# A linear-attention and softplus-MLP kernel: x^T's factor made by Pool, the softplus table loaded first, and a hand-set plan with new positions

## Chip, cores and metric

One core of one Trainium2 chip. The metric is the device time of one execution in microseconds (us). Engines: PE (TensorE, matmuls; PEld are its weight loads), DVE (VectorE), ACT (ScalarE), POOL (GpSimd), SP (SyncE, which here only issues DMA transfers).

## The reference

```python
q, k, v: (8, 8, 576, 64)    g_norm: (64,)    w_in: (512, 2048)    w_out: (2048, 512)
kv  = einsum('bhsd,bhse->bhde', k, v)
out = einsum('bhsd,bhde->bhse', q, kv)
rms = sqrt(mean(out * out, axis=-1, keepdims=True) + 1e-06)
y   = (out / rms * g_norm).astype(float32)
x   = y.transpose(0, 2, 1, 3).reshape(4608, 512)
h   = x @ w_in
g   = maximum(h, 0) + log1p(exp(-abs(h)))          # softplus
return (g @ w_out).astype(float32)
```

The inputs w_in and w_out arrive with twice the width of float32 (64 bits each); the kernel makes float32 of them itself.

## The kernel before

**The two halves.** The attention half works by batch (8) and by tile of 128 tokens (36 tiles). For a batch, `kv_of` loads k and v in four pairs of 256 KB and two tails (L483, L481), multiplies them into one bank of PSUM (L494, "kv group") and copies the result into a block-diagonal tile, kv_diag (L498). For a tile of tokens, `rows` brings q with its rows turned (by PE and an ACT copy for the first two batches, L563 and L570; by DVE from the third on, L538), multiplies with kv_diag (L508, "out_rows"), squares on ACT (L576), sums on DVE (L513), takes the root on POOL (L516, L517) and scales on DVE (L520). The result is turned (L525 on PE for the first 12 tiles) to x^T.

**Three-part numbers.** Every operand of the MLP half is split into three float32r parts, so that three fast matmuls give nearly the exact product. For x^T this is `split`: a high part on ACT (L437, scaled by the column g_down), a low part on DVE (L440, which reads g_col) and a third on DVE (L444). g_col holds g_norm twice, 128 rows; g_down is g_col times a constant near 1.

**Weights.** `weight` loads a chunk of 128 rows or columns of w_in or w_out as raw 64-bit words (512 KB, L275), in one of two raw buffers. ACT squares the high words (L286) to find which are zero, DVE makes float32 of the words in six steps (L290, L294, L299, L307, L312, L316; L299 reads ACT's square, and L312 is the last that reads raw), ACT collects a check sum (L303). `divide` then makes the three parts: high on ACT (L348), low on DVE (L351), low scaled up on ACT (L355), and the third part: for the first four chunks through PE (L366 with ident_r, L367 with minus_r, which is minus the identity, and L370 on ACT), later on DVE and ACT (L358, L362).

**The MLP half** runs over 12 blocks of 384 tokens and 16 chunks of d_ff, in three phases that share the chunks out; 192 steps in all. A step is one h (12 matmuls, L646), softplus and high part on ACT (L666, L668), low and third part on DVE (L657, L661), and three sums of 128 tokens (9 matmuls, L653). At the end of a phase a block's sums go to DRAM or to the output (`leave`).

**What sets the order.** Nothing is ordered by the program's text except the set-up at L725 to L736. All the rest are tasks with an engine, an estimated duration, the tasks they follow, the buffers they take and give, and a position. `Plan.order` plays the program through once on the host with these estimates: at each step it takes, among the tasks that could begin within SOON (150 ns) of the earliest, the one with the lowest position. It starts with all engines free at 0 (`engine_free`) and the transfers free at 0 (`dma_free`). The positions of the early weights, loads and tiles come from the list P0 (its first 8 entries for the conversion of the first chunks, the next 8 for their loads, 11 for the attention half, 13 for later chunks). Every engine then runs its own list strictly in the planned order, and an instruction that waits holds up all that stand behind it on its engine; SP's list of transfers too. Where the plan has PE idle ahead of the first h, it puts in a filler matmul (`warm`, L762), not before BEGIN (4000 ns) of the plan's clock.

**The set-up** before: ACT issues two small loads of g_norm (L726), makes g_down (L727), loads softplus's table (L728) and later makes minus_r (L732). POOL makes an identity, DVE copies it to ident_r (L731) and sets constants (L733 to L736).

Of the kernel before, what the change touches and what calls it, by code (L numbers as in the profile page):

```python
# [13 lines left out]
ALU = mybir.AluOpType  # L14
# [8 lines left out]
DOWN_G = 1.0 - 0.99 * 2.0 ** -13  # L23
# [17 lines left out]
class Plan:  # L41
# [2 lines left out]


    HANDOVER = {"PE": 250, "ACT": 120, "DVE": 120, "POOL": 150, "SP": 0}
    BEGIN = 4000
    SOON = 150

# [17 lines left out]
    def order(self):  # L67
        waiting = {id(t): len(t.after) + (t.follows is not None) for t in self.tasks}
        users = {}
        for t in self.tasks:  # L70
            for a in t.after + ([t.follows] if t.follows else []):
                users.setdefault(id(a), []).append(t)
        ready = {}
        for t in self.tasks:
            if not waiting[id(t)]:
                t.ready = 0
                ready.setdefault(t.engine, []).append(t)
        free = {r: [(0, i) for i in range(n)] for r, n in self.rings.items()}
        engine_free = {"PE": 0, "ACT": 0, "DVE": 0, "POOL": 0, "SP": 0}
        dma_free = 0  # L80
        last_read = {}
        done, left = [], len(self.tasks)
        while left:
            best = None
            for engine, tasks in ready.items():
                options = []
                for t in tasks:
                    at = max(engine_free[engine], t.ready)
                    if t.size:
                        at = max(at, dma_free - 2500)  # L90
                    for i, s in enumerate(t.take):
                        others = sum(u.ring == s.ring for u in t.take[:i])
                        if len(free[s.ring]) <= others:
                            break
                        at = max(at, sorted(free[s.ring])[others][0])
                    else:
                        options.append((at, t))
                if not options:
                    continue
                first = min(at for at, _ in options)  # L100
                at, t = min(((at, t) for at, t in options if at <= first + self.SOON),
                            key=lambda o: (o[1].pos, o[0]))
                if engine == "PE" and self.spare and self.spare[-1].start is None:
                    ring, run, ns, _ = self.spare
                    begin = max(engine_free["PE"], self.BEGIN, min(free[ring])[0] if free[ring] else at)
                    if begin + ns <= at:
                        s = Slot(ring)
                        at, t = begin, Task("PE", ns, lambda s=s: run(s), [], 0.0, [s], [s], 0)
                        s.readers = 1
                if best is None or at < best[0]:  # L110
                    best = (at, t)
            if best is None:
                raise RuntimeError("the plan is stuck at " + str([(e, t.pos, [s.ring for s in t.take if not free[s.ring]]) for e, ts in ready.items() for t in ts][:20]))
            at, t = best
            if t in ready[t.engine]:
                ready[t.engine].remove(t)
                left -= 1
            for s in t.take:
                place = min(free[s.ring])
                free[s.ring].remove(place)  # L120
                s.place = place[1]
            t.start = at
            engine_free[t.engine] = at + t.ns
            t.end = at + t.ns + self.HANDOVER[t.engine]
            if t.size:
                dma_free = max(dma_free, at + t.ns) + t.size
                t.end = dma_free + 2000
            for s in t.give:
                s.readers -= 1
                last_read[id(s)] = max(last_read.get(id(s), 0), t.end)  # L130
                if not s.readers:
                    free[s.ring].append((last_read[id(s)], s.place))
            for u in users.get(id(t), ()):
                waiting[id(u)] -= 1
                if not waiting[id(u)]:
                    u.ready = max([a.end for a in u.after] + ([u.follows.start] if u.follows else []), default=0)
                    ready.setdefault(u.engine, []).append(u)
            done.append(t)
        return sorted(done, key=lambda t: t.start)
# [3 lines left out]
def kernel(  # L143
# [24 lines left out]
    nc = tc.nc  # L168
# [14 lines left out]
    PLACES = 8  # L183
    LAST = PHASES[-1]

    P0 = [-72.5, -0.2, -57.8, -8.7, -11.6, -12.0, -21.4, 2.2, -57.5, -32.8, -36.2, -10.7, -28.2, 0.3,
          -3.2, -2.2, 0.5, -17.5, 12.5, 9.5, 5.5, 6.5, -2.0, 2.5, 2.5, 33.5, 12.5, 14.5, 8.5, 44.5,
          49.5, 68.5, 52.5, 73.0, 96.5, 99.5, 115.5, 110.5, 114.5, 8.5]
    CONVERT, FETCH, EARLY, LATER = P0[:8], P0[8:16], P0[16:27], P0[27:]
    BY_PE = 12  # L190
    AT_ONCE = 2 * TB
# [8 lines left out]
    ident = ident_r.bitcast(F32)  # L200
    minus_r = const.tile([P, P], F32R, name="minus_r")
    g_col = const.tile([P, 1], F32, name="g_col")
    g_down = const.tile([P, 1], F32, name="g_down")
# [520 lines left out]

    for e in range(2):  # L725
        nc.scalar.dma_start(out=g_col[e * D:(e + 1) * D], in_=g_norm.rearrange("(d one) -> d one", one=1))  # L726
    nc.scalar.mul(g_down, g_col, DOWN_G)  # L727
    nc.scalar.preload_act_table_set("softplus")  # L728
    scratch = kv_diag[0][:, 0]
    make_identity(nc, scratch)  # L730
    nc.vector.tensor_copy(ident_r, scratch)  # L731
    nc.scalar.mul(minus_r, ident, -1.0)  # L732
    nc.vector.memset(half, -0.5)  # L733
    nc.vector.memset(big, 2.0 ** 30)
    for x in kv_diag + tails:
# [62 lines left out]
```

## Time and profile before

| | us |
|---|---|
| median of 9 runs (lowest, highest) | 913.12 (912.41, 913.68) |
| the profiled execution's own time | 913.05 |
| its span in the trace | 911.3 |
| PE busy | 898.6 (99%) |
| of it h matmuls (L646, 2304) | 434.3 |
| of it sums (L653, 1728) | 434.1 |
| of it filler (L762, 36) | 15.6 |
| DVE busy | 625.5 (69%) |
| ACT busy | 415.4 (46%) |
| POOL busy | 80.6 (9%) |
| HBM traffic | 143 GB/s over the span |

A line of the timeline has the start, the duration (both in us), the engine, the line of the kernel, the operation, what it writes and reads, the shapes and the count; in brackets how long the engine stood idle before it and what ended that. The windows give, for a stretch, each engine's busy time and count, the granted TensorE clock (1.00 is full), the busy share of the DMA engines (a little over 1 is possible) and GB/s. A line of the waits says who waited for whom, how long in total, how often, and the longest.

### The profile page before, as it was taken

The numbers are of one execution on the slowest core, as the hardware profiler recorded it, in microseconds if no ns is written. First come the engines' busy times: TensorE is split into PE (matmuls) and PEld (weight loads), VectorE is DVE, ScalarE is ACT, GpSimd is POOL, SyncE is SP. The second block draws the span as 40 slices with busy tenths as digits, with TensorE's granted clock in tenths as the row PEclk, the third lists the DMA queues.
The fourth block names the chain that finished last, engine by engine and source line by source line (L and its number), as shares of the span: only waits on it lengthen the run. The fifth ranks groups of instructions, "written<-read, shape, count | busy, mean of one in ns | idle before, by whom it ended". The sixth has DMA issues, their size and how long they took to land.

```text
span 911.3 us, 13889 instructions
## 1 busy us (share of the span) xinstructions
PE 898.6 (99%) x5134; PEld 802.5 (88%) x5134; DVE 625.5 (69%) x1055; ACT 415.4 (46%) x799; POOL 80.6 (9%) x78
## 2 busy tenths in 40 slices
PE   6999999999999999999999999999999999999998
PEld 4788989988889999999999899989999899999997
DVE  5887888775658887688756878888434555555553
ACT  4876556443435557454433545546323333333331
POOL 0333312212123200000000000000000000000000
PEclk7999999999999999999999999999999999999999
DMA  8999999579692644356333454642330433333323
GB/s 229 250 247 255 241 192 223 91 194 169 182 148 64 167 128 139 116 160 200 104 104 127 127 175 139 218 140 94 104 101 4 138 105 105 105 104 105 104 71 103
DMA packets 211444, 131.47 MB, mean 144 GB/s; under 512 B 102320, under 2 KB 185264, under 8 KB 211376
## 3 DMA queue, kind: packets, MB, share of 16 engines
q1 hardware_dynamic: 211216, 130.58, 53.2%
q8 instruction: 40, 0.66, 0.3%
q14 instruction: 28, 0.23, 0.1%
q10 hardware_dynamic: 160, 0.00, 0.0%
HBM read 91.75 MB, written 38.80 MB: 143 GB/s over the span
## 4 chain that ended last, share of the span: by engine, by line
PE 97%; ACT 1%; DVE 1%; DMA 1%; issue 0%; ACTq 0%; DVEq 0%
PE h L646 44%; PE s L653 44%; PE o L508 3%; PE o L494 2%; DMA g_col<-in_g_norm_dram 1%; PE tp L563 1%; PE h L762 0%; PE tp L525 0%; PE h L367 0%; PE s L508 0%; PE h L366 0%; DVE xv L440 0%; DVE m L351 0%; ACT L728 0%; ACT L727 0%
## 5 line engine op out<-in xcount | busy, mean ns | idle before, releaser
L646 PE MATMUL h<-xv,w 128*128 128x384 f32 x2304 | 434.3, 337 | 0.0
L653 PE MATMUL s<-w,gv 128*128 128x512 f32 x1728 | 434.1, 395 | 0.0
L646 PEld LDWEIGHTS h<-xv,w 128*128 128x128 f32 x2304 | 406.6, 188 | 15.1
L653 PEld LDWEIGHTS s<-w,gv 128*128 128x128 f32 x1728 | 319.6, 188 | 59.9 <-issue 0.5
L666 ACT ACTIVATE g<-h 128x384 f32<-128x384 f32 x192 | 94.3, 491 | 396.5 <-PE h L646 388.6
L657 DVE TENSOR_TENSOR gv<-g,gv 128x384 fp32r<-128x384 f32 x192 | 106.7, 556 | 187.2 <-ACT gv L668 186.3
L661 DVE SCALAR_TENSOR_TENSOR gv<-gv 128x384 fp32r<-128x384 f32 x192 | 106.9, 557 | 5.9
L668 ACT ACTIVATE gv<-g 128x384 fp32r<-128x384 f32 x192 | 100.8, 525 | 20.4 <-PE s L653 12.4
L440 DVE SCALAR_TENSOR_TENSOR xv<-m,g_col,xv 128x512 fp32r<-128x512 f32 x102 | 75.8, 743 | 1.3 <-ACT xv L437 1.1
L444 DVE SCALAR_TENSOR_TENSOR xv<-xv 128x512 fp32r<-128x512 f32 x108 | 74.5, 690 | 2.7
L437 ACT ACTIVATE xv<-m,g_down 128x512 fp32r<-128x512 f32 x102 | 70.0, 711 | 3.2 <-DMA m<-x 2.8
L517 POOL TENSOR_TENSOR r<-r,half 128x8 f32<-128x8 f32 x36 | 65.7, 1824 | 3.0
L693 DVE SCALAR_TENSOR_TENSOR m<-s,scale,m 128x512 f32<-128x512 f32 x24 | 17.9, 746 | 30.1 <-PE s L653 30.1
L508 PE MATMUL o<-kv_diag,m 128*128 128x128 f32 (+1 forms) x296 | 37.1, 276 | 0.3 <-ACT kv_diag L498 0.3
L508 PEld LDWEIGHTS o<-kv_diag,m 128*128 128x128 f32 (+1 forms) x296 | 35.0, 179 | 2.4 <-issue 0.9
L516 POOL TENSOR_SCALAR r<-r 128x8 f32<-128x8 f32 x36 | 14.3, 396 | 235.2 <-DVE r L513 235.0
L513 DVE TENSOR_REDUCE r<-x 128x8 f32<-128x512 f32 x36 | 24.4, 679 | 11.3 <-ACT x L576 11.3
L693 DVE SCALAR_TENSOR_TENSOR m<-s,m 128x512 f32<-128x512 f32 x36 | 23.6, 684 | 9.5 <-PE s L653 9.4
L494 PEld LDWEIGHTS o<-m,m 128*64 128x64 f32 x512 | 18.7, 148 | 11.7 <-issue 6.0
L520 DVE TENSOR_TENSOR x<-o,r 128x512 f32<-128x512 f32 x33 | 22.6, 686 | 7.8 <-POOL r L517 7.5
L299 DVE SCALAR_TENSOR_TENSOR m<-sq,m 128x512 f32<-128x512 bf16 x32 | 22.0, 687 | 8.7 <-ACT sq L286 7.4
L303 ACT ACTIVATE sq<-sq,big 128x512 bf16<-128x512 bf16 x32 | 22.9, 716 | 10.0 <-DVE m L299 9.9
(66 smaller groups left out, 436.8 us busy)
## 6 DMA issues: line engine op xcount, KB each, us to landing
m<-x SPq DMA_DIRECT2D x102, 256.0 KB, 4.6
part<-m SPq DMA_DIRECT2D x72, 256.0 KB, 2.7
m<-part SPq DMA_DIRECT2D x72, 256.0 KB, 3.8
raw<-in_moe_w_in_dram SPq DMA_DIRECT2D x16, 512.0 KB, 5.4
m<-in_k_dram SPq DMA_DIRECT2D x32, 256.0 KB, 4.6
m<-in_v_dram SPq DMA_DIRECT2D x32, 256.0 KB, 4.8
raw<-in_moe_w_out_dram SPq DMA_DIRECT2D x16, 512.0 KB, 4.9
qa<-in_q_dram SPq DMA_DIRECT2D x24, 288.0 KB, 6.5
```

The costliest lines, as they stand in the source:

```text
L437: nc.scalar.activation(cols(0, F32R), x.tile, func=AF.Identity, scale=g_down)
L440: nc.vector.scalar_tensor_tensor(out=cols(1, F32R), in0=x.tile, scalar=g_col, in1=cols(0), op0=ALU.mult, op1=ALU.subtract)
L444: nc.vector.scalar_tensor_tensor(out=cols(2, F32R), in0=cols(1), scalar=-RADIX, in1=cols(0), op0=ALU.mult, op1=ALU.add)
L508: nc.tensor.matmul(y[r0:r0 + n, p::NP], lhsT=qT.tile[:, p, r0:r0 + n], rhs=kv_diag[b % 2][:, p].rearrange("r (h d) -> r h d", d=D), start= ...
L517: nc.gpsimd.tensor_tensor(out=r.tile, in0=r.tile, in1=half, op=ALU.pow)
L646: nc.tensor.matmul(hp, lhsT=w_in.tile[:, i, kd * P:(kd + 1) * P], rhs=xv.tile[:, i, kd], start=(m == 0), stop=(m == 3 * KD - 1))
L653: nc.tensor.matmul(mine[i].tile, lhsT=gv.tile[:, m, i * P:(i + 1) * P], rhs=w_out.tile[:, m], start=(c == cs[0] and m == 0), stop=(c == cs ...
L657: nc.vector.tensor_tensor(out=gv.tile[:, 1], in0=g.tile, in1=gv.tile.bitcast(F32)[:, 0], op=ALU.subtract)
L661: nc.vector.scalar_tensor_tensor(out=gv.tile[:, 2], in0=f32[:, 1], scalar=-RADIX, in1=f32[:, 0], op0=ALU.mult, op1=ALU.add)
L666: a = add("ACT", 490, lambda: nc.scalar.activation(new(g, [P, NT]), h.tile, func=AF.Softplus, scale=1.0 + E), [a], s, [g], [h])
L668: a = add("ACT", 530, lambda: nc.scalar.activation(new(gv, [P, 3, NT], F32R)[:, 0], g.tile, func=AF.Copy, scale=DOWN), [a], s, [gv])
L693: a = add("DVE", 700, lambda: nc.vector.scalar_tensor_tensor(out=new(ot, [P, d_model]), in0=bank.tile, scalar=(scale if ph == LAST else 1. ...
```

## The change

Three things: g_down is made by POOL and minus_r by DVE, both of which ACT made before, so that ACT's first instruction behind the two loads is softplus's table; the plan starts with the engines free at the times of READY and the transfers free at 1500 ns, in place of 0; and the list of positions P0 has new numbers.

```diff
+    READY = {"PE": 2500, "ACT": 2500, "DVE": 4000, "POOL": 2500, "SP": 700}
...
-        engine_free = {"PE": 0, "ACT": 0, "DVE": 0, "POOL": 0, "SP": 0}
-        dma_free = 0
+        engine_free = dict(self.READY)
+        dma_free = 1500
...
-    P0 = [-72.5, -0.2, -57.8, -8.7, -11.6, -12.0, -21.4, 2.2, -57.5, -32.8, -36.2, -10.7, -28.2, 0.3,
-          -3.2, -2.2, 0.5, -17.5, 12.5, 9.5, 5.5, 6.5, -2.0, 2.5, 2.5, 33.5, 12.5, 14.5, 8.5, 44.5,
-          49.5, 68.5, 52.5, 73.0, 96.5, 99.5, 115.5, 110.5, 114.5, 8.5]
+    P0 = [-83.5, -6.7, -71.3, -7.7, -12.6, -28.5, -9.9, 1.7, -54.5, -35.3, -53.7, -10.7, -25.7, -1.2,
+          -3.7, -2.2, 0.5, -14.0, 12.5, 9.5, 5.5, 6.0, -2.0, 2.5, 2.5, 19.0, 0.5, 14.5, 8.5, 44.5, 49.5,
+          68.0, 52.5, 73.0, 96.5, 100.0, 115.5, 110.5, 114.0, 8.5]
...
-    nc.scalar.mul(g_down, g_col, DOWN_G)
     nc.scalar.preload_act_table_set("softplus")
     scratch = kv_diag[0][:, 0]
     make_identity(nc, scratch)
     nc.vector.tensor_copy(ident_r, scratch)
-    nc.scalar.mul(minus_r, ident, -1.0)
+    nc.vector.tensor_scalar(out=minus_r, in0=ident, scalar1=-1.0, scalar2=None, op0=ALU.mult)
+    nc.gpsimd.tensor_scalar(out=g_down, in0=g_col, scalar1=DOWN_G, scalar2=None, op0=ALU.mult)
```

In the built program the same tasks stand in another order on every engine for the first part of the run; on PE the two orders are the same from row 627 of 925 on. Up to the first h matmul both hold the same tasks on PE, but for one pair L366/L367 (w_out's first chunk), which the changed kernel has ahead of it and the kernel before behind it. The first kv group has 12 filler matmuls ahead of it, in place of 9; there are 36 in both. On DVE the same tasks stand ahead of the end of tile 2's split. On SP the first ten loads are the same; later the raw load of w_out's third chunk stands behind the second k load of batch 2, in place of behind its third pair.

## The prediction

> **What bounds the kernel now.** I read the page first (busy shares, the granted clock, the chain), then the windows, then the timeline of the first 50 us engine by engine, and last the waits.
>
> ```profile
> PE 898.6 (99%) x5134; PEld 802.5 (88%) x5134; DVE 625.5 (69%) x1055; ACT 415.4 (46%) x799; POOL 80.6 (9%) x78
> 43.80:911.00 867.20, 863.21 (x4846) 777.46 (x4844) 594.90 (x1001) 388.58 (x748) 71.07 (x65) 1.00 0.52 139
> 43.75 2.33 PE L646 MATMUL h<-xv,w 128*128 128x384 f32 x12
> ```
>
> PE sets the end. From its first h matmul (L646, at 43.75) to the last result it is never idle but for the tail of 4 us, and the waits view has no PE wait after 43.8. Its work is the same before and after the change, so time can only come out of the first 43.75 us, or be lost by a new wait behind them. (Columns of windows: length; busy PE, PEld, DVE, ACT, POOL; clock; DMA share; GB/s.)
>
> ```profile
> 7.89 1.28 ACT L727 ACT_TABLE_LOAD   x1 [7.89 <-DMA g_col<-in_g_norm_dram]
> 9.41 1.28 ACT L728 ACT_TABLE_LOAD   x1
> 10.92 0.65 ACT L286 ACTIVATE sq<-raw 128x512 bf16<-128x512 bf16 x1
> 11.60 0.69 DVE L299 SCALAR_TENSOR_TENSOR m<-sq,m 128x512 f32<-128x512 bf16 x1 [5.00 <-ACT sq L286]
> 14.92 0.80 PE L366 MATMUL h<-w,ident_r 128*128 128x512 f32 x1 [0.58 <-ACT w L348]
> 16.58 0.80 PE L367 MATMUL h<-w,minus_r 128*128 128x512 f32 x1 [0.87 <-ACT w L355]
> 17.42 0.60 ACT L370 ACTIVATE w<-h 128x512 fp32r<-128x512 f32 x1
> 19.14 0.69 DVE L351 TENSOR_TENSOR m<-m,w 128x512 f32<-128x512 f32 x1 [0.70 <-ACT w L348]
> ```
>
> This is the hole: ACT stands at g_down's table load until g_col has landed at 7.89, loads two tables, makes g_down and minus_r, and squares the first weight only at 10.92, although DVE had read the same raw tile at 5.45. DVE loses 5.00 us, and the weight chain L299, L316, L348, L351, L355, L366/L367, L370 hangs behind it.
>
> ```profile
> 8.00:10.00 2.00, 0.57 (x11) 0.61 (x13) 0.00 (x0) 1.97 (x3) 0.00 (x0) 0.50 1.10 372
> 12.00:14.00 2.00, 2.00 (x18) 1.35 (x15) 1.90 (x4) 1.50 (x3) 0.00 (x0) 0.50 0.19 65
> 14.00:16.00 2.00, 1.13 (x2) 0.29 (x1) 1.97 (x5) 0.73 (x2) 0.00 (x0) 0.50 0.72 233
> 16.00:18.00 2.00, 1.42 (x13) 0.98 (x15) 1.84 (x4) 1.93 (x4) 0.00 (x0) 0.50 0.88 209
> 20.00:22.00 2.00, 2.00 (x10) 1.25 (x7) 1.83 (x4) 0.49 (x1) 0.00 (x0) 0.59 1.19 310
> 22.00:24.00 2.00, 2.00 (x23) 1.32 (x23) 1.90 (x5) 0.68 (x2) 0.00 (x0) 1.00 1.22 265
> 30.00:32.00 2.00, 2.00 (x26) 1.43 (x24) 1.89 (x4) 1.49 (x4) 1.63 (x3) 1.00 0.29 68
> ```
>
> Two more losses follow from it. PE has half its clock from 8 to about 21.6 (0.59 in the window from 20 is 0.5 + 0.5 x 0.18: full for the last 0.36 us), and gets it back only after the stretch from 18.36 on, in which it had no gap; the gaps before were the waits at L366 and L367. And the DMA engines run nearly dry at 12 to 14:
>
> ```profile
> SPq L275 <- DVE m L312: 5.9, 2, 4.8
> SPq L553 <- PE s L508: 2.5, 1, 2.5
> ```
>
> SP stood 4.8 us (to 13.56) before the third raw load, because L312 had not released raw's buffer, and 2.5 us before a q load (to 29.5), which is the second dry stretch at 30.
>
> **The change part by part.** ACT loses the wait, one table load (1.28), g_down (0.20) and minus_r (0.31). Its remaining load can run at 1.9, when its two DMA issues (0.72 to 1.91) are out, and end at 3.2; so its first square begins when the raw tile is there, 5.45 by DVE's row, in place of 10.92.
>
> The trace shows a price for a table load that differs from the Trainium skill's: "ScalarE: Activation LUTs", section "What ACT_TABLE_LOAD costs", adds a drain of 1.38 us to the 1.28; here the load of 9.41 ends at 10.69 and the next ACTIVATE starts at 10.70. By the page 2.66 us would go instead of 1.28; the sum is the same, since the landing at 5.4 comes last either way.
>
> minus_r goes to DVE: its nearest row is the 128x128 cast at L731, 0.23 us. Cover: DVE waits 1.48 us for the first raw tile before L290; without it, 0.23 would be added to the whole DVE chain. g_down goes to POOL, which waits there for g_col (7.8). Nearest rows are L516's 0.24 to 0.61, so it is ready by 8.5. Behind it on POOL stands only the first root, which had waited until 28.09; its first reader is L437, at 32.96 before. Both at nothing, from 0 to +0.23. READY and the start of dma_free cost nothing themselves; they and P0 move instructions. Both orders hold 36 filler matmuls (L762), all ahead of the first h, but 12 now stand ahead of the first kv group in place of 9. They end near 6.1, and that group waits for v until 9.43 in any case: SP's first ten loads are the same.
>
> Now the walk, with starts from rows and distances between neighbours from the same timeline (DVE: L290 0.46, L294 0.69, L299 0.72, L307 0.47, L312 0.72, L316 0.65; PE at half clock: kv group 1.05, filler 0.59 and then 0.43; at full clock: kv group 0.61, filler 0.31, turn_q 0.41, L366/L367 0.64, out_rows 0.81).
>
> First weight on DVE: L299 6.6, L316 to 9.2 (before 14.2). ACT: L348 at 9.24, DVE L351 10.2, ACT L355 10.9 (before 15.90). Second weight: L316 to 13.3 (before 18.44). Here 5.1 us are won, and then the next thing is late: ACT's L370 stands ahead of the second L348 and needs PE, which goes kv 9.43, two fillers 10.48, kv 11.63, three fillers 12.68, L366 14.2, L367 14.6, all without a wait but still at half clock. So L370 is at 15.35 (before 17.42), L348 at 15.9, L351 at 16.5 (before 19.14): 2.6 us won, with DVE idle from 13.3.
>
> PE now has no gap from 11.6 on. Before, the clock came back 3.3 us after the gapless stretch began (18.36 to 21.64), so I put it at 14.9; the other end is 21.6, as before. With 14.9: kv 15.2, filler, kv 16.1, six fillers to 18.6, turn_q 18.6 (before 23.75), L366/L367 and the tail's kv to 20.3. ACT: L570 19.3, L370 19.9, L303, kv_diag (L498) 21.2 (before 23.92), fourth square 21.9 (26.02). DVE: its L299 22.6 (26.72). PE: out_rows of tile 0 at 22.0 (25.42); ACT L576 23.1; DVE L513 23.75 (27.33); POOL 2.4 to 2.6; L520 at 26.95 (30.72). So the stage is 3.4 to 4.1 us early. From that L299 to the end of tile 2's L444 DVE has the same 25 instructions in both orders, 15.5 us of work in 17.3 (26.72 to 44.01), where its waits were 0.32, 0.39, 0.36 and 0.40. With all that idle time it ends at 39.9, with 0.65 of it at 38.8. First h matmul 4.1 to 5.2 us early; I take 4.6.
>
> On the clock, the rows have it full, half for 13.6 us, then full for good. The Trainium skill ("TensorE: Matmul & The Clock Gate", Part 1) gives the reason and a rule against a fixed date: a free-running window of 3.41 us has to be busy. By it the clock would return between 15.0 and 18.4, a first h up to 1.3 us later than mine.
>
> After the first h the work is given back in part. DMA gains what its dry stretches held: 2.0 x (0.81 + 0.28) = 2.2 us at 12 to 16 for sure, since L312 of the first weight now ends at 8.5 and SP needs no wait; at 30 to 32 another 2.0 x 0.71 = 1.4 if L508 frees q's buffer 3.4 us early. Loads have little to spare later: the k and v of batch 2 issued at 51.65 and 52.31 take 6.1 and 6.9 us (about 59.2), and PE reads them at 60.30. With DMA 2.2 early and 1.1 to spare PE could keep 3.3; with 3.6, all 4.6. I subtract 0.6, about the middle: 4.6 - 0.6 = 4.0. The profiled execution took 913.05 (span 911.3 and 1.75 around it), and the median is 913.12, the same: 913.05 - 4.0 = 909.0.
>
> **The rivals.** (a) The clock comes back as late as before, at 21.6. For it: gaps decide, and kv groups are small matmuls. Then the six fillers run to 20.75 and L366/L367 end about 2.3 later than walked: 4.0 - 2.3 = 1.7, 911.3. Against: the same mix of one kv group and fillers had it back at 21.6.
>
> (b) Transfers bound it. The third w_out chunk's load, 512 KB, now stands ahead of one v half and all later pairs of batch 2. At 372 GB/s (window 8 to 10) it takes 1.4 us: 2.2 + 1.1 - 1.4 = 1.9, 911.2. For it: DMA's share is near 1 from 46 on. Against: the loads behind raw come early as well.
>
> (c) Slower. The same raw load waits for raw's buffer, freed by L312 of the chunk before; SP is in order, so seven k and v pieces, then q, stand behind it, and PE's kv groups block all behind them. It decides the sign when PE loses over 4.0 there. A wait as long as the third load's before, 4.8, on top of its own 1.4 gives 909.0 + 6.2 = 915.2. Against: that L312 ends near 44 in my walk, when SP gets there.
>
> (d) More: twelve fillers keep the clock from falling at 8. Then L370 follows L316 at once, DVE's 3.2 us idle shrinks to below 1, and 4.0 + 2.5 gives 906.5. Against: PE is idle from 6.1 to 9.43 all the same. That the change does not do what it says hardly can be: in ACT's order one table load is left, and the square is its next instruction.
>
> **How the numbers follow.** A run of this kernel can be told from no change at about 0.2%, 1.8 us: faster is below 911.2, slower above 914.9. Chances: forecast 0.53, its own range 907.5 to 910.8; (a) 0.14, (b) 0.12, (c) 0.13, (d) 0.08. Faster: 0.53 + 0.08 + half of (a) and 0.04 of (b) = 0.72; slower 0.13; the same 0.15. The range takes in (d) and the upper half of what lies about (a) and (b), 906.0 to 913.5, and leaves out (c) and the edges.
>
> **What would show it.** First L286 near 5.5, and DVE L299 without its 5.00; L370 near 15.4 and after it DVE's idle 3 us; the clock at 1.00 from 15 to 18; no 4.8 at SP's L275; first h at 38.5 to 39.7. A PE wait after 45 for k, v or raw shows (b) or (c). Wrong I would be most simply if the first h comes early and PE then waits as long, which the order's edits between 45 and 100 us could bring.

## The result, and the profile after

| | before | after |
|---|---|---|
| median of the runs, us | 913.12 (912.09 to 913.90, 30 runs) | 910.07 (909.60 to 912.40, 10 runs) |
| profiled execution, us | 913.05, span 911.3 | 909.43, span 907.6 |
| first h matmul starts, us | 43.75 | 40.29 |
| from there to the end of the span, us | 867.5 | 867.3 |

The ratio of the times is 0.9972, with a 95% interval of 0.9964 to 0.9979: the changed kernel is 3.05 us faster by the medians, 3.62 by the two profiled executions. The profiled execution, 909.43, is below all ten runs of the median, so the profile accounts for 3.6 us and not for what the other runs lost of it. Lines of the code stand one further on than before (L286 is now L287, L370 is L371, L646 is L647).

The page after, its busy shares, and the window from the first h matmul on (columns as in the prediction):

```profile
PE 896.7 (99%) x5134; PEld 802.5 (88%) x5134; DVE 626.1 (69%) x1056; ACT 412.4 (45%) x796; POOL 83.2 (9%) x79
40.30:907.60 867.30, 862.81 (x4845) 777.77 (x4842) 595.10 (x1001) 386.57 (x746) 73.63 (x64) 1.00 0.52 140
```

PE still does as many matmuls and is still busy throughout behind the first h. ACT has three instructions less (two of them, minus_r and g_down, are the one more that DVE and POOL each have; the third is the second table load). In the profile all of the gain lies in front of the first h. The timeline of the first 41 us after:

```profile
1.94 1.28 ACT L728 ACT_TABLE_LOAD   x1 [1.94 <-issue]
5.32 0.68 ACT L287 ACTIVATE sq<-raw 128x512 bf16<-128x512 bf16 x1 [2.10 <-DMA raw<-in_moe_w_in_dram]
6.59 0.69 DVE L300 SCALAR_TENSOR_TENSOR m<-sq,m 128x512 f32<-128x512 bf16 x1
8.15 0.42 POOL L733 TENSOR_SCALAR g_down<-g_col 128x1 f32<-128x1 f32 x1 [6.86 <-DMA g_col<-in_g_norm_dram]
15.45 0.60 ACT L371 ACTIVATE w<-h 128x512 fp32r<-128x512 f32 x1 [3.07 <-PE h L368]
16.59 0.69 DVE L352 TENSOR_TENSOR m<-m,w 128x512 f32<-128x512 f32 x1 [3.15 <-ACT w L349]
18.95 0.60 PE L564 MATMUL tp<-ident_r,qa 128*128 128x128 f32 x4
31.24 0.75 DVE L441 SCALAR_TENSOR_TENSOR xv<-tp,g_col,xv 128x512 fp32r<-128x512 f32 x1 [0.72 <-ACT m L586]
39.07 0.75 DVE L441 SCALAR_TENSOR_TENSOR xv<-tp,g_col,xv 128x512 fp32r<-128x512 f32 x1 [0.56 <-ACT m L586]
40.29 2.33 PE L647 MATMUL h<-xv,w 128*128 128x384 f32 x12
```

One table load is left, and it runs while ACT would wait for the raw tile anyway. POOL now stands for g_col, where ACT stood. L300 no longer waits for the square. Then comes the new wait: L371 stands 3.07 us for PE, and through it DVE 3.15 us at L352. The last two waits shown are DVE's at L441, for ACT's copy L586 of the same turned tile.

The windows that answer to those of before:

```profile
12.00:14.00 2.00, 2.00 (x19) 1.52 (x17) 1.35 (x2) 0.38 (x2) 0.00 (x0) 0.50 1.10 360
14.00:16.00 2.00, 2.00 (x16) 1.16 (x16) 0.00 (x0) 0.55 (x2) 0.00 (x0) 0.51 1.16 167
16.00:18.00 2.00, 2.00 (x30) 1.36 (x26) 1.37 (x3) 1.76 (x4) 0.00 (x0) 1.00 1.07 199
30.00:32.00 2.00, 1.62 (x22) 1.00 (x20) 1.27 (x2) 2.00 (x5) 0.00 (x0) 1.00 0.90 243
```

The two dry stretches of the DMA engines, with shares of 0.19 and 0.29, are filled (1.10 and 0.90). The clock is full again at 16, where before it was half until 21.6. The zeros for DVE and the 0.55 for ACT at 14 to 16 are the new wait.

### The profile page after: what moved, and what is told of

It reads as the page before. It is cut to its first block, busy times and chain, and to the rows that moved or that the text cites. A ratio compares the mean times of both kernels' runs of the same rounds, so it can differ in the third digit from the quotient of the medians.

```text
span 907.6 us, 13880 instructions
## 1 busy us (share of the span) xinstructions
PE 896.7 (99%) x5134; PEld 802.5 (88%) x5134; DVE 626.1 (69%) x1056; ACT 412.4 (45%) x796; POOL 83.2 (9%) x79
## 4 chain that ended last, share of the span: by engine, by line
PE 97%; DMA 2%; ACT 1%; DVE 0%; issue 0%; SPq 0%; DVEq 0%; ACTq 0%
PE s L654 44%; PE h L647 44%; PE o L509 3%; PE o L495 3%; DMA m<-in_v_dram 1%; PE h L763 1%; PE tp L526 1%; DMA m<-in_k_dram 0%; PE tp L564 0%; PE s L509 0%; DMA x<-m 0%; DVE xv L441 0%; PE h L367 0%; ACT xv L438 0%; ACT m L571 0%
## 5 line engine op out<-in xcount | busy, mean ns | idle before, releaser
L647 PE MATMUL h<-xv,w 128*128 128x384 f32 x2304 | 434.5, 337 | 0.0
L647 PEld LDWEIGHTS h<-xv,w 128*128 128x128 f32 x2304 | 406.6, 188 | 15.1
L441 DVE SCALAR_TENSOR_TENSOR xv<-m,g_col,xv 128x512 fp32r<-128x512 f32 x102 | 75.8, 743 | 1.3 <-ACT xv L438 1.3
L438 ACT ACTIVATE xv<-m,g_down 128x512 fp32r<-128x512 f32 x102 | 70.0, 710 | 2.5 <-DMA m<-x 2.0
L352 DVE TENSOR_TENSOR m<-m,w 128x512 f32<-128x512 f32 x30 | 20.5, 684 | 8.8 <-ACT w L349 6.7
```

The source lines that it names most:

```text
L438: nc.scalar.activation(cols(0, F32R), x.tile, func=AF.Identity, scale=g_down)
L441: nc.vector.scalar_tensor_tensor(out=cols(1, F32R), in0=x.tile, scalar=g_col, in1=cols(0), op0=ALU.mult, op1=ALU.subtract)
L647: nc.tensor.matmul(hp, lhsT=w_in.tile[:, i, kd * P:(kd + 1) * P], rhs=xv.tile[:, i, kd], start=(m == 0), stop=(m == 3 * KD - 1))
```

## The experiments

Times are medians, with the lowest and highest and the number of runs; ratios are to the kernel before on the same chip (913.0 to 913.2 in each group).

| run | median, us | ratio, 95% interval | first h, us |
|---|---|---|---|
| e1: set-up alone, on the kernel before | 909.73 (908.97–910.52, 5) | 0.9964 [0.9951, 0.9978] | 39.96 |
| e2: plan alone | 913.20 (912.47–914.21, 11) | 1.0002 [0.9994, 1.0011] | 44.06 |
| e3: no READY, no start of dma_free | 910.98 (909.21–911.53, 7) | 0.9971 [0.9960, 0.9982] | 42.12 |
| e4: positions of before | 909.30 (908.56–909.61, 5) | 0.9957 [0.9945, 0.9970] | 40.30 |
| e5: g_down back on ACT, one table load | 908.85 (908.74–909.67, 5) | 0.9956 [0.9944, 0.9969] | 39.18 |
| e7: first twelve fillers doubled | 910.57 (908.51–912.11, 8) | 0.9972 [0.9962, 0.9982] | 40.35 |
| e8: second weight's L349 ahead of L371 | 908.90 (908.55–911.69, 5) | 0.9956 [0.9942, 0.9970] | 42.92 |
| e10: L441 ahead of L586 | 909.06 (908.50–910.15, 5) | 0.9958 [0.9945, 0.9970] | 41.37 |
| e11: e7 with three raw loads halved | 907.93 (907.64–911.53, 6) | 0.9955 [0.9942, 0.9968] | 38.27 |
| e12: e10, last six fillers doubled | 909.45 (909.27–912.35, 6) | 0.9969 [0.9957, 0.9982] | 40.52 |
| e13: last five fillers left out | 909.87 (908.50–912.02, 5) | 0.9966 [0.9954, 0.9978] | 39.64 |
| e14: two lines of before exchanged | 909.40 (908.32–909.64, 5) | 0.9956 [0.9942, 0.9969] | 40.07 |

### Which part of the change makes the gain: e1 and e2

e1 is the kernel before with only the set-up changed; e2 is the changed kernel with the set-up of before.

```diff
 e1, against before:
-    nc.scalar.mul(g_down, g_col, DOWN_G)
-    nc.scalar.mul(minus_r, ident, -1.0)
+    nc.vector.tensor_scalar(out=minus_r, in0=ident, scalar1=-1.0, scalar2=None, op0=ALU.mult)
+    nc.gpsimd.tensor_scalar(out=g_down, in0=g_col, scalar1=DOWN_G, scalar2=None, op0=ALU.mult)
 e2, against after: the same four lines the other way round
```

> The set-up alone: g_down by POOL, minus_r by DVE, softplus's table first; the plan's start and all positions are those of before, so every engine's order behind the set-up is that of before. Theory (ACT's late start was the loss): the first L286 near 5.4, DVE's L299 without its wait of 5.0, and most of the gain is here: ratio 0.9965 to 0.9980 (2 to 3.2 us less). Rival (the positions bring it): within 1 us of before, ratio 0.999 to 1.001.

> The changed plan (READY, dma_free, P0) with the set-up of before, in which ACT makes g_down and minus_r. Theory: the first square stays near 10.9, and the new order gains nothing by itself: 912 to 914, ratio 0.999 to 1.001. Rival (the positions bring it): 910 to 911, ratio 0.997 to 0.998.

e1 has the whole gain (909.73) and e2 none (913.20). In e1 the first square starts at 5.19 and the first h at 39.96; in e2 the square is at 11.09, L300 waits 5.07 for it, and the first h is at 44.06. So the move of the set-up is the cause, and the new positions are not needed for it. The timeline of e1, then that of e2:

```profile
5.19 0.68 ACT L286 ACTIVATE sq<-raw 128x512 bf16<-128x512 bf16 x1 [1.96 <-DMA raw<-in_moe_w_in_dram]
39.96 2.33 PE L646 MATMUL h<-xv,w 128*128 128x384 f32 x12
```

```profile
11.09 0.65 ACT L287 ACTIVATE sq<-raw 128x512 bf16<-128x512 bf16 x1
11.77 0.69 DVE L300 SCALAR_TENSOR_TENSOR m<-sq,m 128x512 f32<-128x512 bf16 x1 [5.07 <-ACT sq L287]
44.06 2.33 PE L647 MATMUL h<-xv,w 128*128 128x384 f32 x12
```

### What READY and the positions bring: e3 and e4

```diff
 e3, against after:
-        engine_free = dict(self.READY)
-        dma_free = 1500
+        engine_free = {"PE": 0, "ACT": 0, "DVE": 0, "POOL": 0, "SP": 0}
+        dma_free = 0
 e4, against after: P0 of before
```

> The changed kernel, but the plan starts at 0 as before (no READY, dma_free 0). On PE its order differs from the changed kernel's in a few rows only: 33 fillers, 9 of them ahead of the first kv group. Theory: the three fillers are not on the path, so 909.5 to 910.7, the changed kernel's time within 0.5. Rival (fillers keep the clock): half clock for longer behind 8 us, 1 to 2 us more than the changed kernel.

> The changed kernel with the positions of before (set-up and READY stay). On PE the order is that of before but for a few rows: 39 fillers, 12 ahead of the first kv group. Theory: like the set-up alone, 910 to 911. Rival (the new positions carry the gain over the first 100 us): 912 to 913.

Neither is measurably slower than the changed kernel (ratios 0.9971 and 0.9957 beside 0.9972). e3's profiled run, 911.53, is the slowest of its seven: in it PE waited 1.43 us for a half of v at 35.75, and the clock then fell to half from 36.8 to 40.2, which put the first h at 42.12. Three of the seven took 909.2 to 909.8, the other three 911.0 to 911.2. More of this fall below.

### How much of ACT's delay was covered: e5 and e14

e5 is the changed kernel with g_down on ACT again, behind the one table load: ACT waits for g_col, but loads no second table and makes no minus_r. e14 is the kernel before with two lines exchanged, so that softplus's table is loaded ahead of g_down's multiplication; no second load is then needed.

```diff
 e5, against after:
-    nc.gpsimd.tensor_scalar(out=g_down, in0=g_col, scalar1=DOWN_G, scalar2=None, op0=ALU.mult)
+    nc.scalar.mul(g_down, g_col, DOWN_G)
 e14, against before: the line
     nc.scalar.mul(g_down, g_col, DOWN_G)
 moved from ahead of the load of softplus's table to behind it
```

> The changed kernel, but ACT makes g_down again, behind the one load of softplus's table: ACT waits for g_col (landing 7.8 to 7.9) and its first square is at about 8.2 in place of 5.3, half of the 5.5 us given back. Theory (the next bound behind the weight chain is PE at half clock: L371 at 15.45 stands ahead of the second L349): the second weight's L317 ends about 15.7 in place of 13.4, L349 moves from 15.94 to about 16.1, and the time is the changed kernel's within 0.5 (909.5 to 910.6). Rival (the start of ACT goes straight through to the end): half of the gain is lost, 911.3 to 911.8.

> The kernel before with two lines exchanged: softplus's table loaded ahead of g_down, both still by ACT, minus_r by ACT too; plan and positions of before. ACT loses one table load and the second one's place behind the wait, but still waits for g_col to 7.9; its first square is at about 8.5 in place of 10.9. Theory (from the run with g_down on ACT: 2.5 us of ACT's delay are covered by PE's half clock and by the transfers): nearly the whole gain, first h at 39.5 to 41, 909 to 910.5. Rival (each us of ACT's delay counts): 2.4 of 5.5 us won, so 911.3 to 912.

The timeline of e5, then that of e14:

```profile
7.74 0.20 ACT L733 ACTIVATE g_down<-g_col 128x1 f32<-128x1 f32 x1 [4.52 <-DMA g_col<-in_g_norm_dram]
7.85 0.64 ACT L287 ACTIVATE sq<-raw 128x512 bf16<-128x512 bf16 x1
14.37 0.60 ACT L371 ACTIVATE w<-h 128x512 fp32r<-128x512 f32 x1
39.18 2.33 PE L647 MATMUL h<-xv,w 128*128 128x384 f32 x12
```

```profile
1.94 1.28 ACT L727 ACT_TABLE_LOAD   x1 [1.94 <-issue]
7.62 0.20 ACT L728 ACTIVATE g_down<-g_col 128x1 f32<-128x1 f32 x1 [4.40 <-DMA g_col<-in_g_norm_dram]
7.93 0.64 ACT L286 ACTIVATE sq<-raw 128x512 bf16<-128x512 bf16 x1
15.01 0.60 ACT L370 ACTIVATE w<-h 128x512 fp32r<-128x512 f32 x1 [0.62 <-PE h L367]
40.07 2.33 PE L646 MATMUL h<-xv,w 128*128 128x384 f32 x12
```

In both the square is 2.5 to 2.6 us later than in the changed kernel, and nothing is lost by it: L371 is no later (14.37 and 15.01 against 15.45). In the changed kernel it waits 3.07 us for PE, and that wait takes up the delay: 0.62 of it is left in e14, none in e5. (In these two profiles the clock was also back a little earlier, at 14.1 and 15.6.) Of the 5.6 us by which the first square came earlier, the first 3.0 (10.92 to 7.93) bring the whole gain, and the other 2.6 nothing that these runs can tell. e14's 909.40 for an exchange of two lines says what the change was: one table load of 1.28 us is gone, and the other runs at 1.94 in ACT's idle time, where before both stood behind g_col's landing at 7.89. That POOL makes g_down is not needed for it.

### Is the wait at L371 worth something: e8

On ACT the second weight's high part (L349) is put ahead of the first weight's L371; a small function in front of the loop over the plan's order moves the one task and whatever it needs.

```diff
-    for t in plan.order():
+    made = sooner(plan.order(), highs[2], thirds[0])
+    for t in made:
```

> The changed kernel with one ACT instruction moved: the second weight's L349 ahead of the first weight's L371, all other orders as they are. It takes away DVE's wait of 3.15 us at the second L352 (13.4 to 16.6). Theory (ACT's next instructions wait for PE's turn_q at 19 all the same, and the fourth square stays near 22.0): DVE waits as long in front of the fourth weight's L300, first h within 0.5 of 40.3, time within 0.5 of the changed kernel's. Rival (DVE's idle is the bound): first h 2 to 3 us earlier, 907 to 908.

DVE's wait of 3.15 at L352 shrinks to 0.69, but the median gain over the changed kernel is 1.2 us with overlapping intervals, not the 2 to 3 of the rival. Its profiled run is again the slowest of its five (911.69, others from 908.55), with half the clock from 35.5 to 42.3, so its first h of 42.92 does not show what the edit is worth.

### What bounds the stretch now, clock or transfers: e7 and e11

e7 doubles the matmul in each of the first twelve fillers, so that PE has no long gap ahead of the first k and v. e11 is e7 with the third to fifth raw loads halved, the other half filled with zeros by POOL, so that half of these three weight chunks is left out of the computation.

```diff
 e7, against after (in warm):
-        nc.tensor.matmul(new(s, [P, 4, P]), lhsT=ident_r, rhs=ident_r.unsqueeze(1).to_broadcast([P, 4, P]),
-                         start=True, stop=True)
+        fillers.append(s)
+        new(s, [P, 4, P])
+        for _ in range(2 if len(fillers) <= 12 else 1):
+            nc.tensor.matmul(s.tile, lhsT=ident_r, rhs=ident_r.unsqueeze(1).to_broadcast([P, 4, P]),
+                             start=True, stop=True)
 e11, against e7 (in the raw load):
+            if j in (1, 3, 4):
...
+                nc.gpsimd.memset(y[:, rest[0], rest[1]], 0)
+                nc.sync.dma_start(out=y[:, cut[0], cut[1]], in_=src[:, cut[0], cut[1]])
+                return
```

> The changed kernel with two matmuls in each of the first 12 fillers, so that PE is busy until about 8.9 and idle for under 1 us before the first kv group. Theory (half clock between 9 and 16 holds back L371 and turn_q): the clock stays at 1.00, L371 moves from 15.45 to about 13.2, turn_q of tile 0 from 18.95 to about 16.6, and the time falls by 1 to 2 us against the changed kernel (908 to 909). Rival (transfers are the bound by then): the clock stays, but the first h moves by less than 0.5 and the time is the changed kernel's within 0.5.

> The kernel with twice the early fillers (clock at 1.00 throughout), and of the third, fourth and fifth raw load only half is brought, 256 KB in place of 512 (POOL writes zeros in the other half, so half of those three weight chunks is left out of the computation). Theory (with the clock held, transfers are the bound): the waits for raw and qa between 16 and 30 shrink, turn_q of tile 0 moves from 18.0 to about 17.3, the first h from 40.35 to 38.5 to 39.5, and the time falls by 0.8 to 2 us against that kernel's 910.6. Rival (ACT's and DVE's own chain is the bound): first h and time the same within 0.5.

Windows, waits and timeline of e7; the waits' columns are engine, what was waited for, us in total, times, the longest:

```profile
8.00:12.00 4.00, 3.27 (x41) 2.22 (x39) 3.88 (x7) 2.51 (x6) 0.52 (x1) 1.00 1.10 364
12.00:16.00 4.00, 4.00 (x43) 2.49 (x41) 2.08 (x3) 1.55 (x4) 0.00 (x0) 1.00 1.13 253
```

```profile
ACT sq L287 <- DMA raw<-in_moe_w_out_dram: 2.9, 2, 1.7
DVE m L291 <- DMA raw<-in_moe_w_out_dram: 2.1, 2, 1.1
PE tp L564 <- DMA qa<-in_q_dram: 1.3, 1, 1.3
```

```profile
13.28 0.60 ACT L371 ACTIVATE w<-h 128x512 fp32r<-128x512 f32 x1 [0.85 <-PE h L368]
40.35 2.33 PE L647 MATMUL h<-xv,w 128*128 128x384 f32 x12
```

The clock never falls, and L371 runs 2.2 us earlier. The first h is no earlier all the same (40.35 against 40.29), and the median is 910.57: my theory that the clock was worth 1 to 2 us fell. PE, ACT and DVE now wait for q and for raw. Waits and timeline of e11, whose lines stand six further on:

```profile
ACT sq L293 <- DMA raw<-in_moe_w_out_dram: 0.6, 1, 0.6
PE tp L570 <- DMA qa<-in_q_dram: 0.5, 1, 0.5
```

```profile
38.27 2.33 PE L653 MATMUL h<-xv,w 128*128 128x384 f32 x12
```

With fewer bytes the same waits shrink, the first h comes 2.1 us sooner and the median is 2.6 us below e7's, though the intervals of the two just touch (0.9968 and 0.9962) and one run of e11 took 911.53. With the clock held, transfers are thus the next bound of this stretch.

### Three runs on the late fall of the clock: e10, e12, e13

e10 puts L441 ahead of L586 for tiles 0 and 2, to take away the 0.72 and 0.56; e12 is e10 with the last six fillers doubled; e13 is the changed kernel without its last five fillers.

```diff
 e10, against after (copies[t] is the ACT copy L586, lows[t] the task of L441, sooner the function of e8):
-    for t in plan.order():
+    made = plan.order()
+    for t in (0, 2):
+        made = sooner(made, lows[t], copies[t])
+    for t in made:
 e12, against e10 (in warm):
+        for _ in range(2 if len(fillers) > 30 else 1):
 e13, against after (in warm):
+        if len(fillers) > 31:
+            return
```

> The changed kernel with the tasks recorded in another order for tiles 0 and 2: DVE's L441 ahead of ACT's copy L586, which read the same bank of PSUM; the order on each engine stays. In the changed kernel DVE waits 0.72 and 0.56 us for that copy, and PE then 0.42 and 0.48 for L441. Theory (DVE's chain sets the first h): these waits go, ACT's L586 waits in turn, first h 0.5 to 1.2 us earlier than 40.3 and the time 0.4 to 1.0 less than the changed kernel's. Rival (L438 ends last anyway): no change in DVE's start of L441.

> The kernel with L441 recorded ahead of L586, and the last six fillers (between 23 and 37 us) two matmuls each. In that kernel's profile PE waited 1.1 us for v at 35.3, was 54% busy in the clock's window from 33.2, and had half clock from 36.6 to 40.1, with the first h at 41.4. Theory (that fall of the clock is what spreads the times): no half clock behind 16 us, first h at 39.3 to 40.3, times within 1 us of each other, median 908.3 to 909.3. Rival (fillers only push work back): first h later than 40.5, and a median of 909.5 or more.

> The changed kernel without its last five fillers (between 30 and 37 us). Theory (they keep the clock): PE's waits for k, v and q there leave the window from about 33 less than 60% busy, the clock falls for 3.4 us or more behind 36, first h at 41 to 43, and most runs are at 911 to 912.5. Rival (a filler is only work that can be left out): no fall, first h at 39.5 to 40.5, 909 to 910.3.

e10 does not settle its question: the wait at the first L441 goes, others grow (0.93, and 2.19 for tile 2), and its profiled run, the slowest of its five, has this in the timeline and the windows:

```profile
35.30 0.69 PE L498 MATMUL o<-m,m 128*64 128x64 f32 x16 [1.13 <-DMA m<-in_v_dram]
```

```profile
33.00:36.60 3.60, 2.04 (x34) 1.52 (x35) 3.53 (x7) 2.35 (x6) 1.89 (x3) 1.00 0.96 219
36.60:40.00 3.40, 3.40 (x27) 2.77 (x25) 1.18 (x3) 1.61 (x4) 0.43 (x1) 0.51 0.98 267
40.00:43.00 3.00, 2.94 (x25) 2.70 (x22) 2.96 (x6) 2.68 (x6) 0.10 (x1) 0.99 1.02 284
```

PE waits for a half of v, is busy for little over half of the first window, and has half its clock in the next, in which DVE and ACT are busy for only 1.18 and 1.61 of 3.40 us. The theory was that the late fillers keep the clock from this. e12's profile has no fall, but its first h is at 40.52, no earlier than the changed kernel's 40.29, and one of its runs took 912.35; e13 has five fillers less, and its profile has no fall either (908.71, first h 39.64), and four of its five runs took under 910, though another took 912.02. So that theory is not borne out. e13 does not rule a fall out for its slowest run, whose mean granted clock is the lowest of the five (0.992, the others 0.994 to 0.998).

## Why the prediction was right, and where its sizes were off

The forecast was 909.0, with its own range from 907.5 to 910.8; the median is 910.07. Rivals (a), (b) and (c) put the time at 911.3, 911.2 and 915.2, at or beyond the upper end of the interval (0.9979 x 913.12 = 911.2), (d) at 906.5, below its lower end (909.8).

**ACT and the weight chain.** Right: the square at 5.32 (walked 5.45), L317 to 9.2 and 13.4 (9.2 and 13.3), L371 at 15.45 (15.35), L352 at 16.59 (16.5). That L371 stands behind PE and takes back half of the 5.1 us was the step that mattered most; e5 and e14 show it by a square 2.5 us later that costs nothing.

**The clock.** Walked to return at 14.9, and 15.96 measured, inside the two ends. The Trainium skill ("TensorE: Matmul & The Clock Gate", Part 1) has a free-running window of 3.41 us; by it the return was to lie between 15.0 and 18.4, which agrees. The profiles show more of it: each early stretch at half clock is a whole multiple of 3.41 us long, once in e1 (9.35 to 12.76), twice in the changed kernel (9.13 to 15.96), four times before (8.01 to 21.66). In the first 3.41 us of it PE was busy for 0.98 in e1, whose clock came back then, and for 0.87 in the changed kernel, whose clock did not. So the return is not a fixed 3.3 us behind the start of PE's gapless work, as the walk had it (4.2 were measured, from 11.79), and that it came so near 14.9 is luck in part.

What was wrong is its value: rival (a) priced a late return at 2.3 us and (d) a clock that never falls at a gain of 2.5. In e7 it never fell, and nothing was won; PE, ACT and DVE waited for q and raw instead. The kernel before points the same way: of its 48 runs beside the experiments, the 17 with a mean granted clock of 0.996 or more have a median of 912.4 us, the 31 with 0.994 or less one of 913.3. The clocks differ by 0.005 on average, some 9 us at half clock, and the times by 0.9.

**To the fourth square and the first h.** Up to L300 the walk holds: turn_q 18.95 (18.6), kv_diag 21.26 (21.2), square 22.02 (21.9), L300 22.72 (22.6). Then a term was mis-sized. From L300 to the first h I allowed 16.55 us, taking half of DVE's idle time as won; it took 17.57, 1.0 more, and more than the 17.03 of before. DVE's waits at L441 are not won but grow (0.72 and 0.56 against 0.36 and 0.40 before). The first h is 3.46 us earlier, not 4.6.

**The give-back.** I subtracted 0.6 for transfers behind the first h. None was given back there: 867.3 against 867.5 us, and the waits view has no PE wait behind it. The two errors partly cancel: 3.46 + 0.2 in the profile against 4.6 - 0.6. That is luck, and the 3.05 of the medians is a further 0.6 below it.

**The DMA gain.** "2.2 us for sure" was wrong. From before to after, the third raw load lands at 15.84 in place of 17.25, the fourth at 20.52 for 21.58, the fifth at 27.88 for 27.92: 1.4, 1.1 and nothing, though the dry stretches were filled. Only the sixth is 3.3 early (41.03 for 44.38). What paid for the earlier start was the slack of the loads: a half of v of batch 1 landed at 36.38 and was read at 38.40 before; after, it landed at 34.61 and was read at 35.27. That is 0.7 left of 2.0. In e7 one half of v is late: PE waits 1.37 us for it, to 31.04. Rival (b) thus had the right mechanism for the next step, but is not what bounds this change; it starts to in e7, and e11 shows it.

**Priced at nothing, and so measured.** minus_r on DVE, g_down on POOL (ready at 8.6), READY and the positions: e2, e3 and e4 show no cost or gain of the plan's parts that the runs can tell. e5 has g_down on ACT again, e14 both g_down and minus_r, and neither is slower for it. **Rival (c)** is out: SP had no long wait at a raw load (its longest in the first 60 us that is not for g_col is 2.2, at L587), and no PE wait for k, v or raw follows the first h.

**What stays open.** e4, e5, e8, e10 and e14 have medians 0.7 to 1.2 us below the changed kernel's. Their intervals overlap with its own (0.9964 to 0.9979) and with each other, so none is shown to beat it.

## What to carry to other kernels

Look at the first instructions of each engine's queue: a small set-up instruction (g_down is 128x1) that waits for a small load can hold a table load and all real work behind it, and exchanging two lines can be worth the whole change, as e14 shows. Price an earlier start only as far as the next thing that was waiting beside it: here 5.6 us at ACT were 2.6 at DVE's next divide, where PE's queue came last, and 3.5 at the first h. A dry stretch of the DMA engines that gets filled is not that much time won at each later load; follow the landings that somebody reads.

## What the runs showed that was not expected

**A second fall of the clock.** Three of the profiles (e3, e8, e10) have half the clock for 3.4 to 7 us from about 36 on, each after PE had waited 0.9 to 1.4 us for v, and each is the slowest run of its kernel, by 1.6 to 3.1 us over its fastest. Two windows of e3, the second with the fall, and one of e13, behind which there was none:

```profile
33.40:36.80 3.40, 1.57 (x25) 1.22 (x24) 3.33 (x6) 1.99 (x5) 2.47 (x3) 1.00 1.02 227
36.80:40.20 3.40, 3.26 (x25) 2.64 (x25) 0.69 (x1) 1.60 (x4) 0.38 (x1) 0.50 0.96 241
30.20:33.60 3.40, 1.74 (x22) 1.24 (x22) 2.96 (x5) 2.56 (x6) 0.93 (x2) 1.00 1.14 236
```

In e3's first window PE was busy 1.57 of 3.40 us, in pieces. The Trainium skill ("TensorE: Matmul & The Clock Gate", "Why this matters for your kernels") warns of gaps above about 3 us; here the longest wait was 1.43, so several shorter ones are enough. The edges of the windows show in the runs themselves: in each of the three the second fall comes 27.3 us, eight times 3.41, behind the first (9.48 and 36.79 in e3), and lasts 3.41 us or, in e8, 6.83. In the 3.41 us ahead of it PE was busy for 0.46 (e3), 0.54 (e10) and 0.62 (e8). A share of 0.51 in e13's window was not followed by a fall, so the share alone does not decide, and where the limit lies stays open.

Each run's mean granted clock is on record too. Of the kernels whose square is earlier than before, seven have a run above 911.5 us, and in six of them that run has the lowest clock of its kernel (in the changed kernel 912.40 with 0.992, the others 0.995 or more); e3 is the exception. So a late fall is a likely cause of the wide spread (908.5 to 912), but where in those runs the clock was low only a profile would show.

**Two readers of one turned tile take turns.** ACT's L438 and L586 and DVE's L441 all read the tile that PE has turned. DVE's L441 waits for L586, which it needs nothing from; these are the 0.72 and 0.56 above. In e10 L441 goes first and L586 waits for it instead (0.48 at tile 0), so the turn can be changed; what that is worth e10 does not show.
